# Splitting the last PSUM eviction of a decode kernel between ScalarE and VectorE

## The chip, the cores and the metric

The kernel runs on one core of a Trainium2 chip. The metric is the device time of one execution in microseconds (us). In the profile, PE is the matrix engine (TensorE), PEld its weight loads, DVE is VectorE, ACT is ScalarE, and SPq and ACTq are the instruction queues of SyncE and ScalarE from which DMAs are issued. L518 is line 518 of the kernel.

## The reference

One token goes through two branches and a gate mixes the results. The last operations of both branches are products with a weight matrix whose output is 1024 wide; the kernel adds both products in the same PSUM tile.

```python
x = A_x                                          # 1 x 1 x 1024
g = sigmoid((x * gate_w).sum(-1, keepdims=True))
a = attention(x @ wq, k_cache, v_cache) @ wo     # 32 heads, 4 KV heads, 65536 cached keys
z = gelu(x @ w_in); z1, z2 = z[:1792], layernorm(z[1792:])
b = (z1 * (w_sp * z2 + b_sp)) @ w_out            # gMLP branch, shown for one token
return g * a + (1 - g) * b
```

## The kernel before

The kernel streams 162 MB of weights and caches through one large SBUF tile, `kv`. The two output products accumulate in `out_ps`, which has 256 fp32 columns on 128 partitions. Each of the four 32-partition groups (quadrants) holds one quarter of the 1024 outputs, and all 32 partitions of a group hold the same numbers, because the vector is broadcast to 32 columns.

```python
P, B, NB = 128, 32, 4
NO = D // NB                                     # 256
out_ps = psl.tile([P, NO], FP32, name="out_ps")  # 1 KB per partition

def project(w, n, vec, c0, first=False, last=False):
    for c in range(n):
        for t in range(NB):
            nc.tensor.matmul(
                out_ps[t * B:(t + 1) * B, :],
                lhsT=vec[:, c0 + c:c0 + c + 1].to_broadcast([P, B]),
                rhs=w[:, c, t * NO:(t + 1) * NO],
                start=(first and c == 0), stop=(last and c == n - 1),
                skip_group_check=True)
# ... early: project(w_out slice, FC, uT, 0, first=True); then all of attention ...
# last: wo arrives in slices of 16, 8, 4, 2, 1 and 1 rows per partition
        project(t, n, oa, c0, last=(c0 + n == OC))
out_sb = const.tile([P, NO], BF16, name="out_sb")
out_rows = out.rearrange("o t (q n) -> (o t q) n", n=NO)
nc.scalar.copy(out=out_sb[:], in_=out_ps[:])
for i, queue in enumerate((nc.scalar, nc.sync)):
    p0 = (2 * i + 1) * B - 1                     # 31 and 95: two adjacent partitions,
    ins = queue.dma_start(out=out_rows[2 * i:2 * i + 2, :],   # one from each quadrant
                          in_=out_sb[p0:p0 + 2, :])
```

The program framework inserts the semaphore waits between engines; they can be read in the built program. Code for the end barrier and the instruction order is left out; the change doesn't touch it.

Of the kernel before, what the change touches and what calls it, by code (L numbers as in the profile page):

```python
# [28 lines left out]
def kernel(  # L29
# [15 lines left out]
    nc = tc.nc  # L45
# [187 lines left out]
    for t in range(2):  # L233
        nc.vector.tensor_tensor(
            out=xm[:, t], in0=xb_ps[:, t * P:(t + 1) * P].rearrange("p (i c) -> p c i", c=KC),
# [52 lines left out]
    for hf in range(2):  # L288
        nc.vector.tensor_tensor(  # L289
            out=zm[:, hf], in0=z_ps[:, hf * HN:hf * HN + ZN].rearrange("p (j c) -> p j c", c=FC),  # L290
# [3 lines left out]
                            in_=zm.rearrange("p h j c -> p h c j"), axis=AX.X, op=ALU.add)  # L294
# [44 lines left out]
    for k in range(NHB):  # L339
        xs = slice(k * NX // NHB, (k + 1) * NX // NHB)  # L340
        nc.vector.tensor_tensor(  # L341
            out=qm[:, xs], in0=q_ps[:, k * HN:(k + 1) * HN].rearrange("p (x j e) -> p x j e",
                                                                   j=B, e=2),
# [6 lines left out]
        out=q4[:], in0=q1[:].rearrange("p x e -> p (x e)").unsqueeze(1).to_broadcast(  # L350
            [P, NB, NX * 2]),
# [7 lines left out]
    for g in range(G):  # L359
        k, t0 = g * T2 // NB, g * T2 % NB  # L360
        nc.vector.tensor_copy(out=qs[:, g].rearrange("p b (t h) -> p b t h", t=T2),
                              in_=qv[:, k, t0:t0 + T2].rearrange("p t h b -> p b t h"))
# [106 lines left out]
    NO = D // NB  # L469
    out_ps = psl.tile([P, NO], FP32, name="out_ps")  # L470
# [44 lines left out]
            c0 += n  # L515
    out_sb = const.tile([P, NO], BF16, name="out_sb")
    out_rows = out.rearrange("o t (q n) -> (o t q) n", n=NO)
    nc.scalar.copy(out=out_sb[:], in_=out_ps[:])  # L518
    for i, queue in enumerate((nc.scalar, nc.sync)):
        p0 = (2 * i + 1) * B - 1  # L520
        ins = queue.dma_start(out=out_rows[2 * i:2 * i + 2, :], in_=out_sb[p0:p0 + 2, :])
# [40 lines left out]
```

## Time and profile before

| | before |
|---|---|
| time, median of 3 runs | 383.5 us (383.31 to 383.65) |
| span of the profiled run | 381.7 us |
| load queue, share of the DMA engines' span | 98.7% |
| PE, DVE, ACT busy | 60%, 57%, 10% |
| the edited copy | 0.372 us |

These lines of the page of the kernel before give the busy time of each engine with its share of the span, and the queue that loads. The load queue's packets take 98.7% of the DMA engines' span, so the stream of loads bounds the kernel.

```profile
PE 229.4 (60%) x1372; PEld 56.6 (15%) x796; DVE 218.4 (57%) x211; ACT 39.6 (10%) x55; POOL 4.4 (1%) x10
...
q1 hardware_dynamic: 4324, 162.01, 98.7%
```

The chain of waits that ended last, for the kernel before, from 365 us on. The columns are the start, the duration, and what the time went to.

```profile
347.56 31.38 DMA kv<-in_A_wo_dram
378.94 0.04 issue
378.98 0.32 PE out_ps L475 x4
379.30 0.02 issue
379.32 0.37 ACT out_sb L518
```

The timeline of the same run shows what follows. The columns are start, duration, engine, line and operation; the bracket gives the idle time before it and what ended it.

```profile
379.32 0.37 ACT L518 CAST out_sb<-out_ps 128x256 bf16<-128x256 f32 x1 [45.57 <-PE out_ps L475]
379.72 0.32 SPq L521 DMA_DIRECT2D out_dram<-out_sb  x1
379.73 0.25 ACTq L521 DMA_DIRECT2D out_dram<-out_sb  x1
```

After the last load everything is serial: four matmuls, one copy, two output DMAs, and 1.98 us from the DMA's issue at 379.72 to the end of the span at 381.7. From the start of the copy to the first issue is 379.72 - 379.32 = 0.40 us. The change acts on this stretch alone.

### The profile page before, as it was taken

To read this page: it belongs to the slowest core of one execution; us is meant where nothing else is said; L and a number is where in the kernel's file an instruction comes from. 1 tells how busy PE (TensorE), PEld (TensorE's weight loads), DVE (VectorE), ACT (ScalarE), POOL (GpSimd) and SP (SyncE) were. 2 spreads that over 40 slices of the span, in tenths; PEclk is the share of its full clock that TensorE was granted. 3 is DMA by queue.
4 is the path that set the end of the run, shared out by engine and by line. 5 is a ranking of instruction groups with operands and counts; after the bars stand their busy time and mean duration, and the time that the engine had idled before them with its cause. 6 is when DMAs were issued, how large, how long until landed. Compare 5 with 4: busy or idle time off the path is not lost.

```text
span 381.7 us, 2586 instructions
## 1 busy us (share of the span) xinstructions
PE 229.4 (60%) x1372; PEld 56.6 (15%) x796; DVE 218.4 (57%) x211; ACT 39.6 (10%) x55; POOL 4.4 (1%) x10
## 2 busy tenths in 40 slices
PE   0433465678157934796379539762977196749355
PEld 0110011112011200121011101110111011212123
DVE  4241487996689306966996058669860497550040
ACT  1010001111601100114011001140100010500000
POOL 4000000000000000000000000000000000000000
PEclk9996569998669885989598958995889599969768
DMA  9999999999999999999999999999999999999995
GB/s 376 438 419 422 433 435 440 433 471 415 407 426 440 440 441 426 440 433 440 440 428 440 440 440 433 434 427 426 412 433 441 433 440 413 428 419 433 433 414 220
DMA packets 4376, 162.17 MB, mean 425 GB/s; under 512 B 521, under 2 KB 525, under 8 KB 909
## 3 DMA queue, kind: packets, MB, share of 16 engines
q1 hardware_dynamic: 4324, 162.01, 98.7%
q8 instruction: 8, 0.13, 0.1%
q14 instruction: 4, 0.02, 0.0%
q10 hardware_dynamic: 40, 0.01, 0.0%
HBM read 162.01 MB, written 0.00 MB: 424 GB/s over the span
## 4 chain that ended last, share of the span: by engine, by line
DMA 60%; PE 20%; DVE 15%; issue 1%; ACT 1%; SPq 1%; DVEq 0%; ACTq 0%
DMA kv<-in_A_k_cache_dram 38%; PE s_ps L388 15%; DVE kv L381 9%; DMA kv<-in_A_wo_dram 8%; DMA kv<-in_A_wq_dram 7%; DMA kv<-in_A_v_cache_dram 7%; PE o_ps L434 3%; DVE pt L424 2%; DVE mx L383 1%; DVE o_sb L448 1%; PE q_ps L274 1%; ACT sc L421 1%; DVE rowt L444 1%; ACT sc L399 1%; SPq L165 1%
## 5 line engine op out<-in xcount | busy, mean ns | idle before, releaser
L388 PE MATMUL s_ps<-kv,wt 128*128 128x512 bf16 x512 | 138.1, 427 | 85.4 <-DVE kv L381 85.4
L381 DVE STREAM_TRANSPOSE kv<-kv 128x2048 int32<-128x2048 int32 x64 | 142.7, 2280 | 58.8 <-DMA kv<-in_A_k_cache_dram 58.8
L434 PE MATMUL o_ps<-kv,pt 128*64 128x512 bf16 x512 | 62.6, 404 | 7.5 <-DMA kv<-in_A_v_cache_dram 7.5
L388 PEld LDWEIGHTS <-wt 128*128 128x128 bf16 x256 | 27.1, 106 | 197.7 <-issue 133.8
L399 ACT CAST sc<-s_ps 128x1024 bf16<-128x1024 f32 x16 | 16.2, 1013 | 253.0 <-PE s_ps L388 253.0
L434 PEld LDWEIGHTS <-pt 128*64 128x64 bf16 x256 | 16.2, 116 | 51.3 <-issue 48.4
L424 DVE STREAM_TRANSPOSE pt<-sc 128x1024 bf16<-128x1024 bf16 x16 | 18.6, 1217 | 6.8 <-ACT sc L421 6.8
L444 DVE TENSOR_TENSOR rowt<-o_ps,own 128x1024 f32<-128x1024 f32 x4 | 4.8, 1195 | 25.7 <-PE o_ps L434 25.7
L421 ACT ACTIVATE sc<-sc,nb 128x1024 bf16<-128x1024 bf16 x16 | 18.2, 1137 | 12.2 <-DVE nb L417 12.2
L383 DVE TENSOR_REDUCE mx<-sc 128x1 f32<-128x1024 bf16 x12 | 14.5, 1206 | 7.0 <-ACT sc L399 7.0
L454 PE MATMUL om_ps<-o_sb,hsel 128*32 128x128 f32 x8 | 2.5, 421 | 19.7 <-DVE o_sb L448 19.7
L403 DVE TENSOR_REDUCE mx<-sc 128x1 f32<-128x1024 bf16 x4 | 4.9, 1220 | 13.6 <-ACT sc L399 13.6
L274 PE MATMUL q_ps<-kv,xT 128*32 128x512 bf16 x64 | 7.2, 630 | 7.3 <-DMA kv<-in_A_wq_dram 7.3
L274 PE MATMUL z_ps<-kv,xT 128*32 128x448 bf16 x64 | 6.4, 577 | 3.9 <-DMA kv<-in_B_w_in_dram 3.9
L475 PE MATMUL out_ps<-kv,oa 128*32 128x256 bf16 x128 | 6.5, 364 | 3.3 <-DMA kv<-in_A_wo_dram 1.9
L341 DVE TENSOR_TENSOR rowt<-q_ps,own_b 128x512 f32<-128x512 f32 x2 | 1.3, 686 | 12.4 <-PE q_ps L274 12.4
L448 DVE TENSOR_REDUCE o_sb<-rowt 128x128 f32<-128x1024 f32 x4 | 7.5, 1872 | 0.1
L289 DVE TENSOR_TENSOR rowt<-z_ps,own_b 128x448 f32<-128x448 f32 x2 | 1.2, 620 | 8.6 <-PE z_ps L274 8.6
L274 PEld LDWEIGHTS <-xT 128*32 128x32 bf16 x64 | 3.0, 139 | 19.3 <-issue 19.3
L230 PE MATMUL xb_ps<-xg,spread 8*128 8x256 bf16 x1 | 0.4, 367 | 9.0 <-DMA xg<-in_gate_w_dram 9.0
L475 PEld LDWEIGHTS <-oa 128*32 128x32 bf16 x128 | 4.5, 129 | 5.5 <-issue 2.7
L518 ACT CAST out_sb<-out_ps 128x256 bf16<-128x256 f32 x1 | 0.4, 372 | 45.6 <-PE out_ps L475 45.6
(88 smaller groups left out, 54.9 us busy)
## 6 DMA issues: line engine op xcount, KB each, us to landing
kv<-in_A_k_cache_dram SPq DMA_DIRECT2D x4, 4096.0 KB, 26.8
kv<-in_A_wq_dram SPq DMA_DIRECT2D x2, 4096.0 KB, 32.9
kv<-in_A_v_cache_dram SPq DMA_DIRECT2D x2, 4096.0 KB
kv<-in_B_w_in_dram SPq DMA_DIRECT2D x2, 3584.0 KB, 15.1
kv<-in_A_wo_dram SPq DMA_DIRECT2D x1, 4096.0 KB
kv<-in_B_w_out_dram SPq DMA_DIRECT2D x1, 3584.0 KB
kv<-in_A_wo_dram SPq DMA_DIRECT2D x1, 2048.0 KB, 28.1
kv<-in_A_wo_dram SPq DMA_DIRECT2D x1, 1024.0 KB, 30.2
```

The source lines that it names most:

```text
L274: ins = nc.tensor.matmul(ps[t * B:(t + 1) * B, k * HN:k * HN + n], lhsT=xT[:, i * KH + c:i * KH + c + 1].to_broadcast([P, B]), rhs=w[:, c, ...
L381: nc.vector.transpose(out=kb[:, v * n:(v + 1) * n], in_=kb[:, v * n:(v + 1) * n])
L383: nc.vector.reduce_max(**late.pop())
L388: ins = nc.tensor.matmul(s_ps[:, k * HN:(k + 1) * HN], lhsT=wt[g % 2][:, v, b].rearrange("p a v h -> p (a v h)"), rhs=kx[:, b // 2, b % 2, ...
L399: nc.scalar.copy(out=sct[g, j][:], in_=s_ps[:])
L403: nc.vector.reduce_max(**late.pop())
L421: nc.scalar.activation(out=sct[g, j][:], in_=sct[g, j][:], func=ACT.Exp, scale=SCALE, bias=nb[:, 0:1], accum_out=lss[g][:, j:j + 1])
L424: nc.vector.transpose(out=ptt[g, j][:].rearrange("p c x -> p (c x)"), in_=sct[g, j][:])
L434: ins = nc.tensor.matmul(o_ps[g][hs, e, :], lhsT=ptt[g, j][:, 2 * u:2 * u + 2, :].rearrange("p c x -> p (c x)"), rhs=vx[:, 2 * u + e], sta ...
L444: nc.vector.tensor_tensor(out=om8, in0=o_ps[g][:].rearrange("p e (v d) -> p (e v) d", d=DH), in1=own_8[:].unsqueeze(2).to_broadcast([P, 2 ...
L448: nc.vector.tensor_reduce(out=o_sb[:], in_=om8.rearrange("p x d -> p d x"), axis=AX.X, op=ALU.add)
L475: nc.tensor.matmul(out_ps[t * B:(t + 1) * B, :], lhsT=vec[:, c0 + c:c0 + c + 1].to_broadcast([P, B]), rhs=w[:, c, t * NO:(t + 1) * NO], st ...
```

## The change

The intent is to halve the last copy by letting ScalarE and VectorE work on it at once.

```diff
-    nc.scalar.copy(out=out_sb[:], in_=out_ps[:])
+    nc.scalar.copy(out=out_sb[:, :NO // 2], in_=out_ps[:, :NO // 2])
+    nc.vector.tensor_copy(out=out_sb[:, NO // 2:], in_=out_ps[:, NO // 2:])
```

## The prediction

> **What bounds the kernel now.** The page of the profile gives the load queue 98.7% of the DMA engines' span (424 GB/s over 381.7 us), while PE is busy 60%, DVE 57% and ACT 10%. The chain of waits from 365 us on has only five pieces: the wait for the last wo slices until 378.94 us, an "issue" piece of 0.04, four out_ps matmuls of 0.32, 0.02, and the ACT copy out_sb<-out_ps of 0.37 at 379.32. The timeline shows the two output DMAs issued at 379.72 and 379.73, and the span ends at 381.7: about 1.7 us of landing and closing that nothing here touches. So the edited copy is wholly on the critical path, but it is 0.1% of the time. Even a free copy would be "same".
>
> **What the change removes, adds, moves.** It replaces the 128x256 ACT copy by an ACT copy of 128x128 and a DVE copy of 128x128. In the instruction order DVE gains one instruction; nothing else moves. DVE has been idle since about 370.9 us.
>
> The intent is that both run at once; they will not. In the built program the ACT half waits for PE as before, but the DVE half waits for the ACT semaphore at the count which the ACT half reaches, and both output DMAs wait for DVE alone. out_ps is 128x256 fp32, 1 KB in each partition[...]. [...]
>
> **Cost.**
> - ACT half: 128x1024 fp32 from PSUM took 1013 ns, 128x256 took 372, so 0.835 ns a column and 158 fixed: 265 ns for 128. Saved: about 107 ns.
> - ACT to DVE hand-over: from the copy's end to the DMA issue took 0.03 to 0.04 us; I estimate 40 ns.
> - DVE half: DVE reads of PSUM took 161 ns at 128x2 and 184 at 128x32 (copies), 267 at 32x128 (a multiply); I estimate 280 ns. [...]
> Sum: 265 + 40 + 280 = 585 ns in place of 372: **+0.21 us**, all on the critical path.
>
> **Predicted time.** 383.5 + 0.2 = 383.7 us. The three runs before span 0.34 us[...], so the range is 382.9 to 384.5. Chances: faster by over 2% 0.005, within 2% 0.99, slower by over 2% 0.005.
>
> **What would show it.** In the timeline after the last four matmuls: an ACT copy of about 265 ns, then a DVE copy of about 280 ns that starts after the ACT copy ends and whose releaser is named as ACT, then both output DMAs about 0.6 us after the matmuls instead of 0.40. The chain of waits gains a DVE out_sb piece. Wrong would be: the two copies overlapping (then the end moves about 0.1 us earlier), or a DVE copy of over 400 ns.
>
> **What would make it wrong.** A different HBM or DMA rate in the run, which shifts the arrival of the last wo slice by more than the 0.2 us; a wrong hand-over; or a slower closing barrier.

Four passages are cut from this text, where the marks stand, because no run here shows what they said of the hardware: two gave a reason for the wait between the engines, one a second estimate of the DVE half, and one a drift of the time. The sum: 265 + 40 + 280 = 585 ns in place of 372, or +0.21 us. The 280 ns are an estimate from the three DVE times named beside it, and the range of 382.9 to 384.5 us is the author's estimate.

## The result, and the profile after

| | before | after |
|---|---|---|
| time, median of 6 runs | 383.56 us (383.31 to 383.75) | 383.64 us (383.51 to 383.78) |
| mean of the 6 | 383.53 us | 383.64 us |
| span of the profiled run | 381.7 us | 382.0 us |

The ratio is 1.0003, with a 95% interval of 0.999 to 1.0016: the same. A ratio is the mean time of one kernel's fast runs over that of the other's fast runs of the same rounds, so it is not quite the ratio of the medians. All runs were fast ones, which means here that none lay more than 1.5% above the fastest of its kernel. The total time alone doesn't tell whether the change did anything.

The trace does. The timeline of the changed kernel's tail:

```profile
378.94 0.41 PE L475 MATMUL out_ps<-kv,oa 128*32 128x256 bf16 x4 [0.25 <-DMA kv<-in_A_wo_dram]
...
379.39 0.27 ACT L518 CAST out_sb<-out_ps 128x128 bf16<-128x128 f32 x1 [45.30 <-PE out_ps L475]
379.69 0.29 DVE L519 CAST out_sb<-out_ps 128x128 bf16<-128x128 f32 x1 [9.31 <-ACT out_sb L518]
380.01 0.32 SPq L522 DMA_DIRECT2D out_dram<-out_sb  x1
380.01 0.25 ACTq L522 DMA_DIRECT2D out_dram<-out_sb  x1
```

The DVE half starts only when the ACT half has ended (379.39 + 0.27 = 379.66), and its bracket names ACT as what it waited for. From the start of the first copy to the issue is now 0.62 us in place of 0.40. The chain of waits of the changed kernel agrees: it has two pieces, 0.27 and 0.29, where one of 0.37 stood.

```profile
378.90 0.04 issue
378.94 0.43 PE out_ps L475 x4
379.37 0.02 issue
379.39 0.27 ACT out_sb L518
379.67 0.02 issue
379.69 0.29 DVE out_sb L519
```

The 0.3 us between the two profiled spans can be laid out from these lines. The last load arrived 0.04 us earlier (378.90 against 378.94), the four matmuls took 0.11 longer (0.43 against 0.32), the copies 0.22 longer, and the time from the issue to the end is the same (1.99 against 1.98). The matmuls' part is not the change's doing. From 376.0 to 378.9 us the granted clock (the share of TensorE's full clock, as the profile gives it) was 1.00 in the run of before and 0.78 in this one. In a second profile of the changed kernel (e12 below) the same matmuls took 0.29 us in the timeline, as in the kernel before, where this profile has 0.41.

The wait is in the built program. This is the end of each engine's instruction order in the changed kernel, with the engine that each instruction's semaphore belongs to:

```
ACT  TensorCopy out_sb<-out_ps 128x128     waits PE
DVE  TensorCopy out_sb<-out_ps 128x128     waits Activation
ACT  DMACopy    out_dram<-out_sb 2x256     waits DVE
SP   DMACopy    out_dram<-out_sb 2x256     waits DVE
```

### The profile page after: what moved, and what is told of

Read it like the earlier page. It is cut to its first block, busy times and chain, and to the rows that moved or that the text cites. A ratio compares the mean times of both kernels' runs of the same rounds, so it can differ in the third digit from the quotient of the medians.

```text
span 382.0 us, 2587 instructions
## 1 busy us (share of the span) xinstructions
PE 232.8 (61%) x1372; PEld 56.9 (15%) x796; DVE 218.7 (57%) x212; ACT 39.5 (10%) x55; POOL 4.4 (1%) x10
## 4 chain that ended last, share of the span: by engine, by line
DMA 60%; PE 22%; DVE 14%; issue 1%; ACT 1%; SPq 1%; DVEq 0%; ACTq 0%
DMA kv<-in_A_k_cache_dram 37%; PE s_ps L388 17%; DMA kv<-in_A_wo_dram 8%; DVE kv L381 8%; DMA kv<-in_A_wq_dram 7%; DMA kv<-in_A_v_cache_dram 7%; PE o_ps L434 3%; DVE pt L424 2%; DVE mx L383 1%; DVE o_sb L448 1%; PE q_ps L274 1%; ACT sc L421 1%; DVE rowt L444 1%; ACT sc L399 1%; SPq L165 1%
## 5 line engine op out<-in xcount | busy, mean ns | idle before, releaser
L388 PE MATMUL s_ps<-kv,wt 128*128 128x512 bf16 x512 | 142.3, 438 | 81.7 <-DVE kv L381 81.7
L434 PE MATMUL o_ps<-kv,pt 128*64 128x512 bf16 x512 | 61.7, 399 | 7.6 <-DMA kv<-in_A_v_cache_dram 7.6
L421 ACT ACTIVATE sc<-sc,nb 128x1024 bf16<-128x1024 bf16 x16 | 18.2, 1137 | 12.2 <-DVE nb L417 12.2
```

Source lines behind the costliest of these rows:

```text
L388: ins = nc.tensor.matmul(s_ps[:, k * HN:(k + 1) * HN], lhsT=wt[g % 2][:, v, b].rearrange("p a v h -> p (a v h)"), rhs=kx[:, b // 2, b % 2, ...
L421: nc.scalar.activation(out=sct[g, j][:], in_=sct[g, j][:], func=ACT.Exp, scale=SCALE, bias=nb[:, 0:1], accum_out=lss[g][:, j:j + 1])
L434: ins = nc.tensor.matmul(o_ps[g][hs, e, :], lhsT=ptt[g, j][:, 2 * u:2 * u + 2, :].rearrange("p c x -> p (c x)"), rhs=vx[:, 2 * u + e], sta ...
```

## Experiments

Theory A: the two halves are serial because both read one PSUM bank, for which the framework orders the engines, and the whole 0.22 us is on the critical path. Rivals: B, they are serial because both write one SBUF tile; C, the loss is only a second fixed cost, whatever the order of the engines; D, the tail is hidden by something else, so that its 0.22 us never reaches the total. The built program lists where tiles lie: `out_ps` in bank 7, the second tile of e2 from bank 0 on. The halves also share one PSUM tile, which A doesn't tell apart from the bank; that is taken up under "Built only".

e1 to e4 ran once each beside one run of the kernel before (383.72 us). Their totals, 384.18, 383.63, 383.64 and 383.59 us, are single runs of unknown state, so only their traces are used as evidence.

### e1: two SBUF tiles, one PSUM bank

```diff
-    out_sb = const.tile([P, NO], BF16, name="out_sb")
+    out_sb = const.tile([P, NO // 2], BF16, name="out_sb")
+    out_sb2 = const.tile([P, NO // 2], BF16, name="out_sb2")
...
+    nc.scalar.copy(out=out_sb[:], in_=out_ps[:, :NO // 2])
+    nc.vector.tensor_copy(out=out_sb2[:], in_=out_ps[:, NO // 2:])
+    for i, (queue, t) in enumerate(((nc.scalar, out_sb), (nc.sync, out_sb2))):
+        ins = queue.dma_start(out=out_rows[:, i * NO // 2:(i + 1) * NO // 2], in_=t[0:P:B, :])
```

> Both halves still read one PSUM bank, but write two SBUF tiles, each sent by its own queue (4 rows of 128 columns). Theory A (the DVE half waits for the ACT half because both read one PSUM bank): the wait stays; DVE copy of about 290 ns starts 0.30 us after the ACT copy starts, releaser ACT; the later output DMA is issued about 0.62 us after the ACT copy starts, the ACT queue's at about 0.30. Rival B (it waits because both write one SBUF tile): the two copies start within 0.05 us of each other and both DMAs are issued by 0.35 us. The built program already shows the wait on the ACT semaphore, so A is expected.

The timeline of e1's tail:

```profile
379.37 0.27 ACT L519 CAST out_sb<-out_ps 128x128 bf16<-128x128 f32 x1 [45.33 <-PE out_ps L475]
379.67 0.61 ACTq L522 DMA_DIRECT2D out_dram<-out_sb  x1
379.67 0.29 DVE L520 CAST out_sb<-out_ps 128x128 bf16<-128x128 f32 x1 [9.34 <-ACT out_sb L519]
379.99 0.63 SPq L522 DMA_DIRECT2D out_dram<-out_sb  x1
```

The wait on ACT stays though the halves share no SBUF tile, and the second DMA is issued 0.62 us after the first copy starts. Rival B falls. One thing was not expected: an output DMA's issue took 0.61 and 0.63 us in place of 0.25 and 0.32, and the single run took 384.18 us against 383.72 for the kernel before. That is taken up in e9 and e10.

### e2: two PSUM banks

The right 128 columns accumulate in a second bank. The second tile takes space of the score tiles, which are free by the end. The early part of the sum (the w_out product) stays in `out_ps`; its right half is saved to SBUF early and added by the instruction that evicts the right half.

```diff
+        right.append(pss.tile([P, 2 * HN], FP32, name="out_ps2", tag="s"))
...
+                nc.tensor.matmul(out_ps[ts, :m], lhsT=lhsT, rhs=w[:, c, t * NO:t * NO + m], ...)
+                if not first:
+                    same_weights(nc.tensor.matmul(
+                        right[0][ts, :NO // 2], lhsT=lhsT, rhs=w[:, c, t * NO + m:(t + 1) * NO], ...))
+        if first:
+            nc.vector.tensor_copy(out=part[:], in_=out_ps[:, NO // 2:])
...
-    nc.vector.tensor_copy(out=out_sb[:, NO // 2:], in_=out_ps[:, NO // 2:])
+    nc.vector.tensor_tensor(out=out_sb[:, NO // 2:], in0=right[0][:, :NO // 2], in1=part[:],
+                            op=ALU.add)
```

> The right 128 columns accumulate in a second PSUM bank (the earlier part of the sum, from uT, is kept in SBUF and added by the DVE instruction that evicts the right half); one SBUF tile as in the changed kernel. Theory A: ACT and DVE start within 0.05 us of each other, ACT about 265 ns, DVE (a tensor-tensor add of 128x128 from PSUM, 286 ns elsewhere in the trace) about 290 ns, both DMAs about 0.32 to 0.36 us after the copies start, against 0.40 before and 0.62 in the changed kernel. Rival B (SBUF tile): still 0.62 us. The last slice's matmuls are twice as many, half as wide, so PE may take 0.0 to 0.2 us longer. Total time 383.4 to 383.8, not resolvable from before.

The result is correct. The timeline of e2's tail:

```profile
379.46 0.27 ACT L530 CAST out_sb<-out_ps 128x128 bf16<-128x128 f32 x1 [45.56 <-PE out_ps L487]
379.50 0.29 DVE L531 TENSOR_TENSOR out_sb<-out_ps,part 128x128 bf16<-128x128 f32 x1 [8.79 <-PE out_ps L487]
379.85 0.33 SPq L535 DMA_DIRECT2D out_dram<-out_sb  x1
379.86 0.26 ACTq L535 DMA_DIRECT2D out_dram<-out_sb  x1
```

With neither the bank nor the PSUM tile shared any longer, and the SBUF tile still shared, both engines run at once and each waits for PE alone. So it is what the halves share in PSUM that makes them wait, as A says. The second bank came with a second tile, though, so this run doesn't show which of the two the framework goes by. The gain is small. DVE starts 0.04 us after ACT, takes 0.29, and the DMAs, which now wait for two engines, start 0.06 us after its end. The sum is 0.39 us: 0.03 to 0.07 more than I expected, and only 0.01 below the one ACT copy of before. The copies win 0.08 us, and the later start of the second engine and the wait for both give nearly all of it back. (In e8 below, where each DMA waits for one engine, it starts 0.02 to 0.03 us after that engine's copy.)

### e3: both halves on ACT

```diff
-    nc.vector.tensor_copy(out=out_sb[:, NO // 2:], in_=out_ps[:, NO // 2:])
+    nc.scalar.copy(out=out_sb[:, NO // 2:], in_=out_ps[:, NO // 2:])
```

> Both halves by ACT, one after the other, no hand-over between engines. If the loss in the changed kernel is only that a second fixed cost is added (158 ns of fixed cost each), ACT start to DMA issue is about 0.56 us (2 x 265 + 0.03); if consecutive ACT instructions overlap, less: about 0.46 us. [...]

A sentence on what makes up the rest of the 0.62 us is cut from this expectation, as no run had shown it; the measured parts are below. An overlap of consecutive ACT instructions is in the trace of the kernel before: L421's ACTIVATE started at 99.82 us and took 1.15, and the next instruction started at 100.88, 0.09 us before its end.

The timeline of e3's tail:

```profile
379.42 0.27 ACT L518 CAST out_sb<-out_ps 128x128 bf16<-128x128 f32 x1 [44.92 <-PE out_ps L475]
379.58 0.27 ACT L519 CAST out_sb<-out_ps 128x128 bf16<-128x128 f32 x1
379.88 0.33 SPq L522 DMA_DIRECT2D out_dram<-out_sb  x1
```

The second copy starts 0.16 us after the first, well before the first ends, so two instructions on one engine overlap and the stretch is 0.46 us. The overlap is 0.27 - 0.16, about 0.10 us before rounding. So of the 0.22 us, a second instruction costs 0.06 when it stays on ACT; the other 0.16 (0.62 - 0.46) comes from putting it on the other engine behind a semaphore. There the 0.10 us of overlap is lost, the hand-over adds 0.03, and the DVE half is 0.03 longer than the ACT half. Rival C explains only the smaller part.

### e4: half of the copy left out (a wrong result)

```diff
-    nc.scalar.copy(out=out_sb[:], in_=out_ps[:])
+    nc.scalar.copy(out=out_sb[:, :NO // 2], in_=out_ps[:, :NO // 2])   # right half: zeros, set early
```

> Wrong result on purpose: only the left half is copied, by ACT; the right half of the SBUF tile is zeros, set early. This is the most that a perfect split could give: ACT copy 265 ns, DMA issue 0.30 us after its start, against 0.40 before, so a gain of 0.10 us; total within 0.3 us of before (383.2 to 383.7). All theories agree on the copy; if the total fell by far more, the tail would hold something else.

The result was wrong, as intended. The copy started at 379.54 and the DMAs were issued at 379.83: 0.29 us, 0.11 less than before. One run took 383.59 us beside 383.72 for the kernel before, a difference within the spread of the runs. This is the ceiling of the idea: half an ACT copy costs 265 of the whole copy's 372 ns, because the fixed part is 158 ns (an estimate, from 372 ns for 256 columns and 1013 ns for 1024).

### e5, e6, e7: the tail made 17 times larger

A tenth of a microsecond can't be told from the spread of the runs. Repeating the eviction 17 times over the same data makes it measurable and tests rival D. The three kernels below repeat the changed kernel's pair, the kernel before's whole copy, and the two-bank pair of e2. Their results are correct.

```diff
+    for _ in range(17):
         nc.scalar.copy(out=out_sb[:, :NO // 2], in_=out_ps[:, :NO // 2])
         nc.vector.tensor_copy(out=out_sb[:, NO // 2:], in_=out_ps[:, NO // 2:])
```

> The changed kernel's pair of half copies done 17 times over the same data (result unchanged). Theory A (serial by the bank, all on the critical path): each of 16 extra pairs takes 265 + 30 + 292 + 30 = about 0.62 us, so 383.6 + 9.9 = 393.5 us, ratio about 1.026, slower. Rival (the two halves overlap in truth, or the tail is covered by something else): below 388.5 or no change.

> The whole copy of before done 17 times by ACT (result unchanged); each waits for the one before it. Theory A: 372 + 30 = 0.40 us each, 16 extra: 383.5 + 6.4 = 389.9 us, ratio 1.017. It must lie some 3.5 us below the 17 pairs of halves if each pair costs 0.22 us more than a whole copy.

> The halves in two PSUM banks, each engine repeating its own half 17 times, no wait between the engines. Theory A: set by DVE, 290 + 30 = 0.32 us each, 16 extra: 383.4 + 5.1 = 388.5 us, ratio 1.013, about 1.4 us below the 17 whole copies and 5 below the 17 pairs in one bank. Rival (the engines slow one another when both read PSUM): at or above the whole copies' 389.9.

| repeated 17 times | expected | median of 4 runs | ratio to before, 95% interval |
|---|---|---|---|
| pair of halves, one bank (e5) | 393.5 us | 393.68 us | 1.0265 (1.025 to 1.028) |
| whole copy on ACT (e6) | 389.9 us | 389.94 us | 1.0167 (1.0152 to 1.0183) |
| pair of halves, two banks (e7) | 388.5 us | 388.67 us | 1.0134 (1.0119 to 1.0149) |

All three ran on one chip, beside 7 runs of the kernel before (median 383.5 us). The first repetitions of e5 in its timeline:

```profile
379.23 0.27 ACT L519 CAST out_sb<-out_ps 128x128 bf16<-128x128 f32 x1 [45.55 <-PE out_ps L475]
379.53 0.29 DVE L520 CAST out_sb<-out_ps 128x128 bf16<-128x128 f32 x1 [9.04 <-ACT out_sb L519]
379.85 0.27 ACT L519 CAST out_sb<-out_ps 128x128 bf16<-128x128 f32 x1 [0.36 <-DVE out_sb L520]
380.15 0.29 DVE L520 CAST out_sb<-out_ps 128x128 bf16<-128x128 f32 x1 [0.33 <-ACT out_sb L519]
```

The engines take turns: each one's bracket names the other, and a pair takes 0.62 us. The same stretch of e7's timeline, where the 17 repetitions of each engine are merged into one line:

```profile
379.33 5.01 ACT L531 CAST out_sb<-out_ps 128x128 bf16<-128x128 f32 x17 [44.92 <-PE out_ps L487]
379.37 5.49 DVE L532 TENSOR_TENSOR out_sb<-out_ps,part 128x128 bf16<-128x128 f32 x17 [10.18 <-PE out_ps L487]
```

The two lines run side by side. The 17 whole copies of e6 follow one another on ACT:

```profile
379.30 6.83 ACT L519 CAST out_sb<-out_ps 128x256 bf16<-128x256 f32 x17 [45.55 <-PE out_ps L475]
```

A turn is 6.83 / 17 = 0.40 us, one copy's 372 ns and 0.03 more. In the built program each copy waits for the one before it, and the overlap of e3 is not there.

In e7 a DVE half takes 5.49 / 17 = 0.32 us a turn, with no sign that the engines slow each other when they read different banks: a single instruction is 291 ns of DVE here, and 265 ns of ACT, where the changed kernel, with one engine after the other, has 292 (a copy) and 265.

Each of the 17 pairs of e5 differs from each of the 17 whole copies of e6 by (393.67 - 389.93) / 17 = 0.220 us, from the means of the runs. This is the cost of the change, measured in total time, and it equals the 0.22 us read from the two traces and the +0.21 us of the prediction. Rival D falls: what is added to the tail reaches the total. In e5 the stretch from the first copy to the SP queue's issue is 389.81 - 379.23 = 10.58 us, 10.18 more than the 0.40 before, and the mean total is 10.19 above that of the kernel before. By the same sum a pair in two banks is (389.93 - 388.66) / 17 = 0.075 us cheaper than a whole copy, with the doubled matmuls of its kernel included. That holds for many turns, where the later start of DVE and the wait for both engines are paid once; a single pair gains 0.01 us, as e2 showed.

### e8: a candidate to beat both

Two banks as in e2, and two SBUF tiles with a DMA each as in e1, so that no engine waits for the other.

> Candidate to beat both: two banks, two SBUF tiles, each engine's half sent by a DMA of 4 rows x 128 columns that waits for that half alone. Expected in the trace: ACT's DMA issued 0.30 us after the copies start, SP's 0.33 us (0.40 before, 0.62 changed); total 383.4, ratio 0.9995 to 1.000, class same, not resolvable from before in time. If PE's doubled matmuls in the last slice cost 0.1 us or more, nothing is won.

This missed. The median of 4 runs is 384.06 us against 383.5 for the kernel before (ratio 1.0016, interval 0.9999 to 1.0032). The timeline of e8's tail:

```profile
379.25 0.27 ACT L531 CAST out_sb<-out_ps 128x128 bf16<-128x128 f32 x1 [44.70 <-PE out_ps L487]
379.29 0.29 DVE L532 TENSOR_TENSOR out_sb<-out_ps,part 128x128 bf16<-128x128 f32 x1 [9.43 <-PE out_ps L487]
379.55 0.61 ACTq L535 DMA_DIRECT2D out_dram<-out_sb  x1
379.60 0.63 SPq L535 DMA_DIRECT2D out_dram<-out_sb  x1
```

The copies and the starts of the DMAs came out close to what was expected (0.30 and 0.35 us after the first copy, for 0.30 and 0.33). The doubled matmuls cost nothing that shows: from the start of the last slice's matmuls to the first copy it is 379.25 - 378.91 = 0.34 us, and 379.32 - 378.98 = 0.34 in the kernel before. But each DMA takes 0.6 us to issue, as in e1, and the span ends 2.6 us after the last DMA's start (382.2 - 379.60), where the kernel before needs 1.98.

### e9, e10: the form of the output DMA by itself

e9 is the kernel before with its single copy, and with the output DMAs of e8: 4 rows of 128 columns from partitions 0, 32, 64 and 96. e10 keeps 2 rows of 256 columns but takes them from partitions 32 apart in place of adjacent ones.

```diff
 # e9
-        ins = queue.dma_start(out=out_rows[2 * i:2 * i + 2, :], in_=out_sb[p0:p0 + 2, :])
+        cs = slice(i * NO // 2, (i + 1) * NO // 2)
+        ins = queue.dma_start(out=out_rows[:, cs], in_=out_sb[0:P:B, cs])
 # e10
+        ins = queue.dma_start(out=out_rows[2 * i:2 * i + 2, :],
+                              in_=out_sb[2 * i * B:2 * (i + 1) * B:B, :])
```

> The kernel before, its single ACT copy kept, but each output DMA takes 4 rows of 128 columns (partitions 0, 32, 64, 96) in place of 2 adjacent rows of 256. If it was the form of the output DMA that cost the candidate (e8) its gain: issue 0.61 and 0.63 us in place of 0.25 and 0.32, and a total of 383.9 to 384.2, 0.4 to 0.6 us over the kernel before. Rival (the doubled matmuls or the two banks cost it): issue and total as before, 383.5.

> The kernel before with each output DMA still 2 rows of 256 columns, but from partitions 32 apart (0 and 32; 64 and 96) in place of adjacent ones. If the distance of the partitions makes the issue long: 0.6 us and 383.9 to 384.2 in total. If the number or the width of the rows does: issue 0.25 and 0.32 us and 383.5 as before.

e9 took 384.13, 384.31 and 384.39 us, at or a little above the expected 383.9 to 384.2, and a fourth run took 389.37. That run, which is the profiled one, had a mean granted clock of 0.728 where the others had 0.821 to 0.854; it is 1.4% above the fastest, and I leave its total aside (the reported ratio of 1.0053 includes it). Its issue times, 0.62 and 0.63 us, are as in e8. e10 took 384.16 us (median of 4; ratio 1.0016, interval 1.0003 to 1.003) beside 383.55 for the kernel before. The timeline of e10's tail:

```profile
379.16 0.37 ACT L518 CAST out_sb<-out_ps 128x256 bf16<-128x256 f32 x1 [45.57 <-PE out_ps L475]
379.56 0.61 SPq L521 DMA_DIRECT2D out_dram<-out_sb  x1
379.57 0.59 ACTq L521 DMA_DIRECT2D out_dram<-out_sb  x1
```

With the same two rows of the same width, only from partitions 32 apart, the issue takes 0.59 to 0.61 us in place of 0.25 to 0.32, and the total rises by about 0.6 us. So it is the choice of partitions, not the number or width of the rows, that cost e8 more than its copies could win. The longer issue is only part of that cost. By the packet times in the traces, the first packets of the two output DMAs move 0.74 and 0.78 us after their issues in the kernel before, and 1.20 and 1.47 us in e10; from the last packet to the end of the span it is about 1.1 us in both. The added time thus lies between the issue and the packets. The reason is not shown. Whether it is the distance, or where the rows start, these runs don't separate. The odd-looking partitions 31, 32 and 95, 96 of the kernel before were well chosen.

### e11, e12: the two-bank kernel and the changed kernel, timed closely

> The two-bank kernel again, to see whether its shorter tail (copy start to DMA issue 0.39 us with a stagger of 0.04, against 0.40 before and 0.62 changed) shows in the time: mean 0.0 to 0.1 us below the kernel before, 0.15 to 0.3 us below the changed kernel of this call. If the last slice's matmuls give it back, equal to before.

> The changed kernel again in the same rounds: mean 0.15 to 0.3 us above the kernel before (serial copies, +0.22 us on the critical path). If it is not above, the tail's 0.22 us is hidden by something after the output DMAs, which the 17-fold runs speak against.

On one chip, the means are 383.53 us for the kernel before (9 runs), 383.69 for the changed kernel (5 runs) and 383.50 for the two-bank kernel (5 runs). The changed kernel is 0.16 us above before and 0.18 above the two-bank kernel; from the spread of the runs the standard error of either difference is 0.05 to 0.06. The two-bank kernel is 0.02 us below before, which is no difference (standard error 0.06). In its second profile the two halves again ran at once. In the second profile of the changed kernel the copy started at 379.18 and the DMAs at 379.80: 0.62 us again.

### Built only

A split by partitions (ACT the first 64, DVE the other 64) was built but not run. Its halves touch different quadrants of the bank, and the DVE half still waits on ACT in the built program. One more program was built, and not run: e8 with both halves accumulated in one PSUM tile that spans two banks, each engine reading a bank of its own. There the DVE half waits on ACT too. So in these builds the framework's wait goes with the PSUM tile that two engines read, and separate banks or quadrants within one tile don't lift it; e2 was free of the wait because its right half had a tile of its own. Two tiles in one bank were not tried. Whether halves in different quadrants run at full speed side by side stays open, and so does what happens when both engines read one PSUM tile at once: no program without the wait was run.

## Why the prediction was right

- **What bounds the kernel.** Right. The load stream fills the span, the copy is on the critical path but 0.1% of it, and even leaving half of the copy out (e4) moved the trace by 0.11 us.
- **The two halves do not run at once.** Right, and shown: the DVE half's releaser is ACT. The wait was read in the built program, so this was no luck. The kernel before even held such a pair: on DVE, L252 reads the same PSUM tile as L251 on ACT, and it started at 13.01 us, 0.04 after ACT's end, with ACT named as what it waited for. The reason given, the shared PSUM bank, was the author's inference, now cut from the text, and it is not what the runs show: e1 (two SBUF tiles, wait stays) and e2 (a second tile in a second bank, wait gone) place the cause in PSUM, and the build with one tile over two banks, which keeps the wait, points to the tile and not the bank. Why the framework orders two readers of one tile is not shown.
- **Cost of the parts.** The ACT half was predicted at 265 ns and took 265. The hand-over was estimated at 40 ns and took about 0.03 us (379.66 to 379.69). The DVE half was estimated at 280 ns and took 292.
- **The sum.** +0.21 us was predicted; the traces show +0.22, and the 17-fold runs show 0.220 per pair.
- **The time.** 383.7 us was predicted and 383.64 measured. The agreement of the total by itself proves little: the range of 382.9 to 384.5 us would have held no change as well, and the two kernels' first six runs differ by 0.11 us with a standard error of 0.08. The closer timing of e12, 0.16 with a standard error of 0.05, is in line with 0.22 though it doesn't fix it, and the 17-fold runs carry the weight.

What else I got wrong lay in the experiments. e2's copies do overlap, but its stretch was 0.39 us and not 0.32 to 0.36, and e8 was expected at 383.4 us and took 384.06, because I had changed the form of the output DMA without a cost for it.

## What to carry to other kernels

Splitting a PSUM eviction between ScalarE and VectorE gained nothing here while both halves lay in one PSUM tile: the framework ran them one after the other, and the split made the stretch 0.22 us longer, 0.06 for the second instruction and 0.16 for putting it on the other engine behind a semaphore (e3). A second bank helped only with a tile of its own, and then a single split copy won 0.01 us. Look at the waits of the built program before you count on two engines working at once, and ask how much of the instruction is its fixed part (an estimate of 158 of 372 ns here): half of the columns still took 265 ns. To measure a cost that is below the spread of the runs, repeat it many times on the critical path; and when you change where a tail ends, keep the output DMA's form the same, or measure it by itself: other partitions alone cost 0.6 us here (e10).
